# Signs of the weights from a ScalarE slope, first grams in half as many products, and a new order of the steps

## The chip, the cores and the metric

The kernel runs on one core of one Trainium2 chip. The metric is the device time of one execution in microseconds. Three runs of the kernel before gave 718.65, 718.37 and 716.71 us, median 718.37 us.

## The reference

A gated linear attention with a delta rule runs over 768 positions for 4 batches and 8 heads of width 48, and a feed-forward layer follows. Cut to what matters:

```python
def _attn_ref(q, k, v, beta):
    k_n = k / (norm(k, axis=-1, keepdims=True) + 1e-06)
    state = zeros((B, H, D, D))
    for t in range(S):
        kt, vt, bt = k_n[:, :, t], v[:, :, t], beta[:, :, t, None]
        y[:, :, t] = einsum('bhd,bhde->bhe', q[:, :, t], state)
        v_old = einsum('bhde,bhd->bhe', state, kt)
        state = state + bt[..., None] * einsum('bhd,bhe->bhde', kt, vt - v_old)
    return y

def _moe_ref(x, w_in, w_out):          # x: 3072 x 384, from y
    h = x @ w_in                       # w_in 384 x 2048
    g = h * erf(softplus(h))
    return g @ w_out                   # w_out 2048 x 384
```

The weights `w_in` and `w_out` arrive as 64-bit floats; the kernel receives each as a pair of 32-bit words.

## The kernel before, in words

**Attention.** The 768 positions are cut in 12 chunks of 64. For each chunk the kernel forms the grams of the keys (`gram_mm`), scales them by the step sizes and inverse norms of the keys (`norm_ops`, `gram_d`, `gram_a`), inverts the resulting triangular systems (for chunks 0 and 1 on VectorE: `first_blocks`, thirty steps of `first_row`, two transposes in `first_back`; for the others in pairs of chunks on GpSimd: `solve_row`, lines 362 and 363), merges the inverted blocks (`merge_*`) and runs the recurrence, which for each of 48 pairs of chunk and batch is `chain_u`, `chain_s` and `chain_y` on TensorE with copies between them.

**Feed-forward.** Four such pairs make a group of 256 tokens, and there are 12 groups. `x_max`, `x_all` and `x_scale` find the power of two that scales the group, `x_tr`, `x_hi` and `x_lo` split its values into two 16-bit parts. `ffn1` (line 659) multiplies them with the two 16-bit parts of `w_in`, nine products for each of 16 column blocks. Softplus (`e_sp`, line 685) and erf (`e_erf`, line 690) run on ScalarE, each with its own table, and `table` (line 126) issues a table load whenever the other one is wanted. `e_mul`, `e_split` and `e_rest` form the two parts of the product, and `ffn2` (lines 720 to 722) multiplies them with `w_out`. The results of `ffn1` live in two PSUM tiles `ph`; a new one waits until softplus and `h_out` (lines 670, 672) have read the old one.

**Weights.** Each of the two matrices passes through 12 tiles of 128 x 512 numbers. `w_load` brings 512 KB into a tile `raw`, of pairs of words. Of each pair, word 1 holds the sign, the exponent and the upper part of the mantissa, word 0 the rest. `w_mask` (line 536, ScalarE) reads word 1 as a 32-bit float, multiplies by 2^-112 and writes it to a staging place. `w_sign` (line 540, VectorE) keeps only the sign bit in word 1. `w_bits` with k = 0 (line 546, VectorE) shifts the staged word left by 3 and ors the sign in; with k = 1 (line 548, VectorE) it shifts word 0 right by 29 and ors it in. What stands in the staging place is then the weight in 32 bits. `w_sum` (line 553, ScalarE) accumulates magnitudes, `w_max`, `w_all` and `w_scale` make the scale of the matrix from the 12 sums, and `w_hi` (line 587, ScalarE) and `w_lo` (line 596, VectorE) write the two 16-bit parts. `ffn1` can't begin before all 12 tiles of `w_in` have gone through `w_sum`, since one scale serves the whole matrix; `ffn2` likewise needs `w_out`. The tiles `raw` borrow the 5 buffers of `H` and the 7 of `L`, so that twelve can be there at once and a later load waits until a `w_sum` has finished with a buffer.

**The first grams.** For chunks 0 and 1 a gram is wanted as four 32 x 32 blocks, with the blocks of the lower 32 rows in exchanged places. `gram_mm` makes one product for each block, head half and pair: 64 products for half a chunk, 256 for the four half chunks (line 246). Each is two instructions in the trace.

**The order.** The program records 2560 steps with planned times in a list `ev`, sorts them, and then takes them in the order that the table `ORDER` (line 33) gives. Every engine's queue, and the queue of SyncE that issues all loads and stores, is in that order. On TensorE 158 idle products (`warm`, line 141) on a tile of zeros stand in the queue ahead of the first `ffn1`.

## Time and profile before

| what | value |
|---|---|
| median of three runs | 718.37 us |
| the profiled execution: its time | 721.74 us |
| the profiled execution: its span | 720.0 us |
| TensorE busy | 641.5 us (89%) |
| VectorE busy | 512.5 us (71%) |
| ScalarE busy | 439.3 us (61%) |
| GpSimd busy | 387.7 us (54%) |
| first instruction of `ffn1` starts at | 112.89 us |

The span runs from the first instruction of the program to the last, and 1.7 us of the profiled execution lie outside it. The profiled execution is 3.4 us longer than the median. Engines are named PE (TensorE; PEld is its weight load), DVE (VectorE), ACT (ScalarE), POOL (GpSimd) and SP (SyncE); a row's times are microseconds from the start of the span, and what stands in brackets is the idle time of the engine just before and what ended it.

### The profile page before, as it was taken

Reading aid. Unit: us, or ns where it says so; the run is one execution under the profiler, and the core shown is the slowest. Engines: PE = TensorE matmul, PEld = TensorE weight load, DVE = VectorE, ACT = ScalarE, POOL = GpSimd, SP = SyncE. Lnnn points to the kernel's source line nnn. Section 1 sums busy time; section 2 is a strip of 40 time slices with the busy share of each in tenths; the row PEclk is TensorE's granted clock in tenths of the full one; section 3 lists DMA queues with packets and bytes.
Section 4 is the critical chain, followed back from the end, with each engine's and each line's share of the span. In section 5 each row is a group of like instructions: output and inputs, shape, how many; then the busy total and the mean of one; then the engine's idle time right before and its main releaser. Section 6 shows DMA issues by size and latency. Waiting matters only on the chain.

```text
span 720.0 us, 23322 instructions
## 1 busy us (share of the span) xinstructions
PE 641.5 (89%) x10074; PEld 490.9 (68%) x10074; DVE 512.5 (71%) x1053; ACT 439.3 (61%) x694; POOL 387.7 (54%) x540
## 2 busy tenths in 40 slices
PE   4687967796988899999899998999998899999996
PEld 3454645675865777877687776877876677777764
DVE  3599899985778767679568766767594775556562
ACT  1156777784757356576477755746754556867781
POOL 4341279986799823699703887323896331301332
PEclk8678977995999899999999999999999999999999
DMA  9733583152420064620414502506101500000100
GB/s 235 256 113 105 181 232 94 46 101 47 112 80 1 2 133 108 151 51 7 94 39 111 132 1 65 109 18 156 41 6 42 123 25 2 1 25 6 29 23 23
DMA packets 76422, 56.23 MB, mean 78 GB/s; under 512 B 57184, under 2 KB 66528, under 8 KB 76320
## 3 DMA queue, kind: packets, MB, share of 16 engines
q1 hardware_dynamic: 76320, 54.74, 30.5%
q8 instruction: 79, 1.29, 0.8%
q14 instruction: 23, 0.19, 0.1%
HBM read 42.14 MB, written 12.58 MB: 76 GB/s over the span
## 4 chain that ended last, share of the span: by engine, by line
PE 39%; DVE 25%; POOL 16%; issue 7%; ACT 6%; DMA 5%; SPq 1%; POOLq 0%; ACTq 0%; DVEq 0%
PE ph L659 13%; POOL xb L363 6%; POOL tmp L362 6%; PE pr L720 5%; PE pr L722 4%; PE pr L721 4%; DVE H L694 2%; POOL z L447 2%; PE pg L250 2%; PE pc L487 2%; PE pc L460 2%; ACT L126 2%; DVE xl L647 2%; DVE z L466 2%; DVE H L672 1%
## 5 line engine op out<-in xcount | busy, mean ns | idle before, releaser
L659 PE MATMUL ph<-xh,w_in 128*128 128x256 f16 x1152 | 213.5, 279 | 4.9 <-ACT L L685 4.5
L659 PEld LDWEIGHTS <-w_in 128*128 128x128 f16 x1728 | 168.6, 100 | 37.0 <-issue 7.7
L709 POOL TENSOR_TENSOR L<-H,L 128x512 f16<-128x512 f32 x72 | 85.7, 1202 | 175.8 <-DVE L L705 113.5
L659 PE MATMUL ph<-xl,w_in 128*128 128x256 f16 x576 | 160.5, 279 | 1.4 <-DVE xl L647 1.4
L126 ACT ACT_TABLE_LOAD x107 | 137.3, 1283 | 1.9
L722 PE MATMUL pr<-w_out,L 128*128 128x384 f16 x384 | 125.4, 327 | 7.7 <-POOL L L709 7.3
L721 PE MATMUL pr<-w_out,L 128*128 128x384 f16 x384 | 125.4, 327 | 0.4 <-DVE w_out L596 0.4
L720 PE MATMUL pr<-w_out,L 128*128 128x384 f16 x384 | 125.7, 327 | 0.0
L685 ACT ACTIVATE L<-ph,xct 128x512 f32<-128x512 f32 x96 | 65.3, 686 | 83.0 <-DVE H L672 68.9
L363 POOL TENSOR_TENSOR xb<-xb,tmp 128x31 f32<-128x31 f32 (+15 forms) x155 | 99.8, 644 | 12.2
L362 POOL TENSOR_TENSOR tmp<-gb,xb 128x31 f32<-128x31 f32 (+15 forms) x155 | 92.1, 594 | 21.6 <-DMA gb<-d 11.3
L447 POOL TENSOR_TENSOR z<-v,nm 64x192 f32<-64x192 f32 x96 | 56.4, 588 | 75.5 <-DMA v<-vtok 58.0
L694 DVE TENSOR_TENSOR H<-H,L 128x512 f32<-128x512 f32 x96 | 75.9, 801 | 28.0 <-ACT L L690 27.5
L672 DVE TENSOR_SCALAR H<-ph 128x512 f32<-128x512 f32 x72 | 49.0, 684 | 28.1 <-PE ph L659 27.7
L722 PEld LDWEIGHTS <-L 128*128 128x128 f16 x384 | 37.6, 98 | 34.5 <-POOL L L709 8.5
L690 ACT ACTIVATE L<-L 128x512 f32<-128x512 f32 x96 | 57.9, 625 | 0.7
L720 PEld LDWEIGHTS <-L 128*128 128x128 f16 x384 | 37.5, 98 | 21.5
L721 PEld LDWEIGHTS <-L 128*128 128x128 f16 x384 | 37.6, 98 | 20.2
L705 DVE CAST L<-H 128x512 f16<-128x512 f32 x72 | 43.1, 605 | 1.1
L481 DVE TENSOR_TENSOR z<-pc,z 48x192 f32<-48x192 f32 x72 | 25.4, 353 | 23.6 <-PE pc L473 13.7
L141 PE MATMUL warm<-zero 128*128 128x384 f16 x158 | 37.9, 390 | 1.1 <-DVE zero L132 1.1
L642 ACT ACTIVATE xh<-pt,xsx 64x128 f16<-64x128 f32 (+1 forms) x72 | 25.9, 394 | 20.7 <-PE pt L626 12.3
(154 smaller groups left out, 1034.7 us busy)
## 6 DMA issues: line engine op xcount, KB each, us to landing
raw_in<-w_in SPq DMA_DIRECT2D x12, 512.0 KB, 7.3
raw_out<-w_out SPq DMA_DIRECT2D x12, 512.0 KB, 5.7
d<-A SPq DMA_DIRECT2D x20, 256.0 KB, 3.4
kpg<-kT SPq DMA_DIRECT2D x24, 192.0 KB, 3.6
k<-ktok SPq DMA_DIRECT2D x12, 384.0 KB, 3.9
qp<-qT SPq DMA_DIRECT2D x24, 192.0 KB, 3.8
v<-vtok SPq DMA_DIRECT2D x48, 96.0 KB, 3.1
out<-ob SPq DMA_DIRECT2D x48, 96.0 KB, 2.2
```

Source lines behind the costliest of these rows:

```text
L126: se.add_instruction(mybir.InstLoadActFuncSet(name=nc.get_next_instruction_name(), act_func_set_id=i, ins=[], outs=[]))
L362: ge.tensor_tensor(tv, G[:, s, s + 1:].unsqueeze(1).broadcast_to([P, ncol, nr]), Xv[:, :, s:s + 1].broadcast_to([P, ncol, nr]), op=ALU.mult)
L363: ge.tensor_tensor(Xv[:, :, s + 1:], Xv[:, :, s + 1:], tv, op=ALU.add)
L447: ge.tensor_tensor(zz[j % 6][h1, :, hb, :], vt[j][h1], st[c]["nm"][h1, cs].unsqueeze(2).broadcast_to([C, NP, D]), op=ALU.mult)
L659: te.matmul(ph, w[:, i, kt * P:kt * P + P], G[x][:, :, ksl], start=(m == 0), stop=(m == 8))
L685: se.activation(unit("L", g, u), G["ph", u], AF.Softplus, bias=0.0, scale=G["ct"])
L690: se.activation(Lu, Lu, AF.Erf, bias=0.0, scale=1.0)
L694: ve.tensor_tensor(Hu, Hu, unit("L", g, u), op=ALU.mult)
L709: (ge if (g * NFF // EU + u) % GLM else ve).tensor_tensor(G["gl", u], unit("H", g, u), G["gh", u], op=ALU.subtract)
L720: te.matmul(G["po"][a], gh[:, o, asl], wout_h[:, i, :], start=(i == 0), stop=False)
L721: te.matmul(G["po"][a], gh[:, o, asl], wout_l[:, i, :], start=False, stop=False)
L722: te.matmul(G["po"][a], gl[:, o, asl], wout_h[:, i, :], start=False, stop=(i == NFF - 1))
```

## The change

Three things change.

**Signs.** `w_mask` uses the function Prelu in place of Copy, with the same scale and a slope of 2^32 for negative inputs. A negative weight's exponent field then is larger by 32, and that bit becomes the sign bit when the word is shifted left by 3. The word from `w_sign` is no longer needed. A new step `w_low` (VectorE, line 539 of the kernel after) shifts word 0 right by 29 in its place, and one `w_bits` (line 543) shifts the staged word and ors word 0 in. So each of the 24 tiles has two steps on VectorE where it had three; `w_low` reads nothing that ScalarE has made.

**First grams.** For chunks 0 and 1 one product covers both 32-column blocks of a row block; for the lower one it reads its right-hand side with the two blocks exchanged. There are 128 products of 32 x 64 where there were 256 of 32 x 32, 256 instructions in a trace where there were 512.

**Order.** `ORDER` is a new table, of 2536 steps. Lines behind the edits have moved up by 1 to 7.

```diff
-ORDER = (7,14,1,2,3,37,43,5,49,57,23,24,4,32,25,26,28,29,88,30,31,6,65,67,
+ORDER = (14,18,4,80,27,7,12,55,6,36,20,236,9,5,278,52,10,3,11,76,32,48,111,
...
             if name == "pg" and c < 2:
-                for x in range(2):
-                    for f in range(2):
-                        for hb in range(2):
-                            q0 = (1 - hb) * C + f * 32
-                            y = (f ^ x) * 32
-                            te.matmul(pg[q0:q0 + 32, o, x * 32:x * 32 + 32], kf[rd(hb), oo, f * 32:f * 32 + 32], kf[rd(hb), oo, y:y + 32], start=True, stop=True)
+                for f in range(2):
+                    for hb in range(2):
+                        q0 = (1 - hb) * C + f * 32
+                        rhs = kf[rd(hb), oo, :].rearrange("p (y t) -> p y t", y=2)
+                        te.matmul(pg[q0:q0 + 32, o, :].rearrange("p (y t) -> p y t", y=2), kf[rd(hb), oo, f * 32:f * 32 + 32], rhs[:, ::-1, :] if f else rhs, start=True, stop=True)
...
-        se.activation(stage(nm, i), hf, AF.Copy, bias=0.0, scale=2.0 ** -112)
-
-    def w_sign(nm, i):
-        hi = wt[nm]["raw", i][:, :, 1]
-        ve.tensor_scalar(hi, hi, -0x80000000, None, op0=ALU.bitwise_and)
-
-    def w_bits(nm, i, k):
-        raw = wt[nm]["raw", i]
+        se.activation(stage(nm, i), hf, AF.Prelu, bias=0.0, scale=2.0 ** -112, alpha=2.0 ** 32)
+
+    def w_low(nm, i):
+        lo = wt[nm]["raw", i][:, :, 0]
+        ve.tensor_scalar(lo, lo, 29, None, op0=ALU.logical_shift_right)
+
+    def w_bits(nm, i):
         ai = stage(nm, i).bitcast(I32)
-        if k == 0:
-            ve.scalar_tensor_tensor(ai, ai, 3, raw[:, :, 1], op0=ALU.logical_shift_left, op1=ALU.bitwise_or)
-        else:
-            ve.scalar_tensor_tensor(ai, raw[:, :, 0], 29, ai, op0=ALU.logical_shift_right, op1=ALU.bitwise_or)
+        ve.scalar_tensor_tensor(ai, ai, 3, wt[nm]["raw", i][:, :, 0], op0=ALU.logical_shift_left, op1=ALU.bitwise_or)
```

In what follows the order of a queue is shown as rows of line, operation, and what is written from what; numbers behind a name tell tiles of one name apart.

**The start of SyncE's queue.** `kpg` are keys for the first grams, `k` keys for the norms, `raw_in` weights. Before:

```order
L230 DMA kpg_115<-kT 48x1024 x2
L163 DMA k_130<-ktok 128x768
L163 DMA k_135<-ktok 128x768
L230 DMA kpg_141<-kT 48x1024 x2
L169 DMA be_152<-btok 128x32
L173 DMA qp_0_86<-qT 48x1024
L173 DMA qp_1_87<-qT 48x1024
L530 DMA raw_in_461<-w_in 128x1024
```

Now:

```order
L529 DMA raw_in_117<-w_in 128x1024
L230 DMA kpg_119<-kT 48x1024 x2
L230 DMA kpg_124<-kT 48x1024 x2
L529 DMA raw_in_127<-w_in 128x1024
L169 DMA be_130<-btok 128x32
L529 DMA raw_in_133<-w_in 128x1024
L169 DMA be_135<-btok 128x32
L163 DMA k_141<-ktok 128x768
L439 DMA v_143<-vtok 128x192
L529 DMA raw_in_178<-w_in 128x1024
L163 DMA k_180<-ktok 128x768
```

Both loads of `k` stood behind one pair of `kpg`; the second now stands behind two pairs and four tiles of weights.

**The start of VectorE's queue.** L189 sums the squares for the norms, L200 and what follows are the norms themselves. Before:

```order
L132 MEMSET zero 128x192
L189 TENSOR_REDUCE n_0_133<-w_out 128x16 x2
L200 TENSOR_SCALAR n_0_133<-n_0_133 128x32
L202 TENSOR_SCALAR ri_154<-n_0_133 128x32
L203 TENSOR_SCALAR ri_154<-ri_154 128x32
```

Now:

```order
L539 TENSOR_SCALAR raw_in_127<-raw_in_127 128x512
L539 TENSOR_SCALAR raw_in_117<-raw_in_117 128x512
L543 SCALAR_TENSOR_TENSOR w_in<-w_in,raw_in_117 128x512
L539 TENSOR_SCALAR raw_in_133<-raw_in_133 128x512
L132 MEMSET zero 128x192
L539 TENSOR_SCALAR raw_in_178<-raw_in_178 128x512
L543 SCALAR_TENSOR_TENSOR w_in<-w_in,raw_in_133 128x512
L189 TENSOR_REDUCE n_0_257<-w_out 128x16 x2
```

Work on the weights, of which there was none here, stands ahead of the norms. In all, 5 `w_low` and 3 `w_bits` now precede the first transpose (`first_blocks`), where nothing of the weights did.

**VectorE behind the second pair of transposes** (`first_back`, L328 before, L327 now). Before:

```order
L328 STREAM_TRANSPOSE w_out<-w_out 128x32x32
L540 TENSOR_SCALAR raw_in_617<-raw_in_617 128x512
L263 TENSOR_TENSOR w_out<-pr_83,gn_158 128x8x32
L540 TENSOR_SCALAR raw_in_639<-raw_in_639 128x512
L546 SCALAR_TENSOR_TENSOR w_in<-w_in,raw_in_617 128x512
L548 SCALAR_TENSOR_TENSOR w_in<-raw_in_617,w_in 128x512
L540 TENSOR_SCALAR raw_in_528<-raw_in_528 128x512
L548 SCALAR_TENSOR_TENSOR w_in<-raw_in_578,w_in 128x512
L546 SCALAR_TENSOR_TENSOR w_in<-w_in,raw_in_576 128x512
```

Now:

```order
L327 STREAM_TRANSPOSE w_out<-w_out 128x32x32
L262 TENSOR_TENSOR w_out<-pg_0_333,gn_307 128x8x32
L543 SCALAR_TENSOR_TENSOR w_in<-w_in,raw_in_182 128x512
L189 TENSOR_REDUCE n_1_689<-sq_539 128x16
L539 TENSOR_SCALAR raw_in_456<-raw_in_456 128x512
L543 SCALAR_TENSOR_TENSOR w_in<-w_in,raw_in_456 128x512
L539 TENSOR_SCALAR raw_out_387<-raw_out_387 128x512
L353 COPY xm_1_91<-pw_613 16x16x16
```

The next norms (L189) and the copies that the recurrence waits for (L353) come after fewer steps on weights, and a tile of `w_out` is already among these. Between the first transpose and these transposes stood 9 steps on weights (4 of line 540, 3 of 546, 2 of 548) and 2 of line 263; now there are 4 on weights (2 of line 539, 2 of 543). From these transposes to the first `x_max` (line 605; 600 now) there are 42 steps of lines 540 to 548 and 9 of line 596 before, and 33 of lines 539 and 543 and 8 of line 591 now; behind the first `x_lo` (line 647; 642 now) 17 of the former remain before, and 1 now.

On ScalarE, `table` issues 107 loads before and 127 now; 7 of the 20 more fall before the first store of an output tile is prepared, the others are spread over the rest. TensorE has the same 158 products of `warm`, all ahead of the first `ffn1` as before.

More of the change, by code (lines that the diff above doesn't have):

```diff
@@ L866, in delta_ffn_kernel @@
         on(us(tb), w_mask, "in", i)
-        on(us(tb + 0.5), w_sign, "in", i)
-        for k in range(2):
-            on(us(tb + 1 + 0.8 * k), w_bits, "in", i, k)
+        on(us(tb - 0.5), w_low, "in", i)
+        on(us(tb + 1), w_bits, "in", i)
         on(us(tb + 2.8), w_sum, "in", i)
@@ L874, in delta_ffn_kernel @@
         on(t - 0.3, w_mask, "out", i)
-        on(t - 0.2, w_sign, "out", i)
-        for k in range(2):
-            on(t + 0.15 * k, w_bits, "out", i, k)
+        on(t - 0.35, w_low, "out", i)
+        on(t + 0.1, w_bits, "out", i)
         on(t + 0.5, w_sum, "out", i)
```

2 lines of the change are left out of this document (1 added, 1 removed).

## The prediction

> **What bounds the kernel now.** First the page, then busy time by stage, with bounds that the timeline of VectorE gives: the first transpose of `first_blocks`, the end of the second pair of transposes, the first `ffn1`, and the end of VectorE's dense work.
>
> ```profile
> span 720.0 us, 23322 instructions
> PE   4687967796988899999899998999998899999996
> DVE  3599899985778767679568766767594775556562
> 0.00:27.42 27.42, 11.93 (x535) 8.78 (x537) 7.53 (x26) 2.97 (x3) 9.97 (x19) 0.71 0.96 270
> 27.42:51.80 24.38, 21.14 (x411) 14.13 (x413) 23.52 (x46) 11.30 (x19) 10.78 (x11) 0.78 0.41 142
> 51.80:112.90 61.10, 48.81 (x1132) 34.25 (x1124) 56.57 (x123) 46.23 (x103) 26.70 (x38) 0.84 0.60 169
> 112.90:168.00 55.10, 39.94 (x538) 31.55 (x536) 52.15 (x101) 41.62 (x75) 49.95 (x61) 0.90 0.28 60
> 168.00:720.00 552.00, 519.66 (x7480) 402.18 (x7480) 372.75 (x761) 337.13 (x495) 290.32 (x413) 0.97 0.25 57
> ```
>
> The columns behind the window are its length, then busy time (and instructions) of PE, PEld, DVE, ACT and POOL, the granted clock, the DMA share and GB/s. Behind 168 us TensorE is busy 519.66 of 552.00 us, so no other engine is worth much there. Ahead of it VectorE is the bound: 23.52 of 24.38, 56.57 of 61.10, 52.15 of 55.10 us. What TensorE does ahead of 112.9 us is partly idle products. So an earlier end of the front moves everything behind it, as long as TensorE finds its work. These are the places:
>
> ```profile
> 8.15 0.84 ACT L181 ACTIVATE w_out<-k 128x768 f32<-128x768 f32 x1 [1.40 <-DMA k<-ktok]
> 13.97 0.18 DVE L213 TENSOR_SCALAR ga<-gn 128x32 f32<-128x32 f32 x1
> 26.75 0.76 DVE L263 TENSOR_TENSOR w_out<-pg,gn 128x256 f32<-128x256 f32 x2 [4.95 <-PE pg L246]
> 27.42 2.12 DVE L315 STREAM_TRANSPOSE w_out<-w_out 128x1024 f32<-128x1024 f32 x1
> 49.74 2.06 DVE L328 STREAM_TRANSPOSE w_out<-w_out 128x1024 f32<-128x1024 f32 x1
> 114.67 0.37 PE L659 MATMUL ph<-xl,w_in 128*128 128x256 f16 x1 [1.39 <-DVE xl L647]
> ```
>
> Here the first transpose waits for the grams of line 246, not for the norms, which are done at 14 us; and `ffn1` waits for VectorE's `xl`.
>
> ```profile
> 15.34 1.93 PE L246 MATMUL pg<-kpg 48*32 48x32 f32 x128 [7.76 <-issue]
> 20.44 1.93 PE L246 MATMUL pg<-kpg 48*32 48x32 f32 x128 [3.17 <-issue]
> 25.81 0.87 PE L246 MATMUL pg<-kpg 48*32 48x32 f32 x49 [3.44 <-issue]
> ```
>
> The grams' own work is short: 1.93 us for 128 products and as many weight loads, then an idle stretch that ends with nothing but "issue". The starts lie 5.10 and 5.37 us apart while the loads hold 0.96 of the DMA engines, so I read it as instructions that arrive in blocks of 256, one per some 5 us. The Trainium skill, Runtime: NRT & Kernel Launch, section Instruction fetch mechanics, says that fetching goes in blocks of 256 instructions and that crossing one is mostly hidden. The trace agrees with the size and not with the hiding. By that sentence halving the grams would give nothing, by the rows it lifts this wait; my sum stays the same, since term 1 is bounded by a load.
>
> **Term 1, up to the first transpose: 0.4 us lost.** Of the 512 products with their weight loads 512 - 128 - 128 - 49 = 207 ran before the first gap, behind 16 of `warm`: 223 pairs. Now the last gram ends with pair 289 (256 of grams, 33 of `warm`), so one block of 128 pairs is missing, and that came by 15.34 us. The grams are then done near 17 us, ahead of the norms. VectorE's queue gets a wait at its head: the first `w_low` steps wait for tiles of weights, and behind them stand the zeros that `warm` waits for; the first two grams are ahead of `warm` on TensorE, and the others have until the norms are there. But the second `k` stands behind more loads:
>
> ```profile
> raw_in<-w_in SPq DMA_DIRECT2D x12, 512.0 KB, 7.3
> k<-ktok SPq DMA_DIRECT2D x12, 384.0 KB, 3.9
> kpg<-kT SPq DMA_DIRECT2D x24, 192.0 KB, 3.6
> 8.00:10.00 2.00, 0.00 (x0) 0.00 (x0) 0.95 (x1) 0.84 (x1) 0.66 (x2) 1.00 1.09 194
> ```
>
> Up to it: 4 x 512 + 4 x 192 + 2 x 384 and some 130 KB, 3.8 MB. At 270 GB/s (the mean up to 27.42) from about 1.7 us on that is 16 us, at 194 GB/s 21 us. Some of the loads behind it share the engines, so I take 18. From a landing to the last norm step it takes 13.97 + 0.18 - 8.15 = 6.0 us; one `w_low` (0.42), seven steps of 0.38 in place of the last ones, and one `w_bits` (0.69) add 3.8. The transpose starts at 18 + 9.8 = 27.8 in place of 27.42. Ends: 1.6 us gained, 3.4 lost.
>
> **Term 2, to the end of the transposes: 5.6 us gained.** Alone and beside GpSimd, the same step on weights has two prices:
>
> ```profile
> 36.79 0.42 DVE L540 TENSOR_SCALAR raw_in<-raw_in 128x512 int32<-128x512 int32 x1
> 38.30 0.69 DVE L546 SCALAR_TENSOR_TENSOR w_in<-w_in,raw_in 128x512 int32<-128x512 int32 x1
> 40.02 1.28 DVE L548 SCALAR_TENSOR_TENSOR w_in<-raw_in,w_in 128x512 int32<-128x512 int32 x2
> 45.74 2.40 DVE L540 TENSOR_SCALAR raw_in<-raw_in 128x512 int32<-128x512 int32 x2
> 48.05 1.76 DVE L546 SCALAR_TENSOR_TENSOR w_in<-w_in,raw_in 128x512 int32<-128x512 int32 x1
> ```
>
> The stage holds four steps of line 540 (0.42, 0.42, 2.40 for two), three of 546 (0.69, 0.69, 1.76), two of 548 (1.28) and two of line 263 (0.8): 8.5 us. Now it has two `w_low` and two `w_bits`: 2.2 us alone, 5.9 beside GpSimd. GpSimd is busy 10.78 of 24.38 us, so I take 2.9, nearer the first. 5.6 us go; ends 2.6 and 6.3. Everything else in the stage is one serial chain on VectorE, so what goes is gained. The loads of `qp` move behind seven tiles of weights; by the same rates they land near 25 us, where TensorE and GpSimd's masks have until the transposes.
>
> **Term 3, to the first `ffn1`: 8 us gained.** The means of the steps by shape:
>
> ```profile
> L540 DVE TENSOR_SCALAR raw_in<-raw_in 128x512 int32<-128x512 int32 x12 | 8.5, 716 | 0.0
> L540 DVE TENSOR_SCALAR raw_out<-raw_out 128x512 int32<-128x512 int32 x12 | 6.8, 566 | 0.1
> L546 DVE SCALAR_TENSOR_TENSOR w_in<-w_in,raw_in 128x512 int32<-128x512 int32 x12 | 9.6, 802 | 0.2
> L546 DVE SCALAR_TENSOR_TENSOR w_out<-w_out,raw_out 128x512 int32<-128x512 int32 x12 | 10.6, 888 | 0.1
> L548 DVE SCALAR_TENSOR_TENSOR w_in<-raw_in,w_in 128x512 int32<-128x512 int32 x12 | 8.6, 724 | 0.1
> L548 DVE SCALAR_TENSOR_TENSOR w_out<-raw_out,w_out 128x512 int32<-128x512 int32 x12 | 11.2, 961 | 0.1
> ```
>
> `w_low` has the shape and stride of line 540 and takes its price. Up to `x_max` the old queue has, for `w_in`, 8 of line 540, 9 of 546 and 10 of 548, and for `w_out` 5 of each: 20.2 + 12.1 = 32.3 us. The new one has 5 `w_low` and 7 `w_bits` of `w_in`, 11 and 10 of `w_out`: 9.2 + 15.1 = 24.3. So 8 us less, and 9.1 with the two steps of line 540 that also go between `x_max` and `x_lo`. ScalarE is the next limit: its queue has about the same 46 us of work here, so 61.1 us can become 52 only with ScalarE at 89% busy; I take 8, ends 4 and 9.1.
>
> **Term 4, 112.9 to 168 us: 5 us gained.** Of steps on weights, 17 become 1: by the means of `w_out`, 4 x 0.57 + 5 x 0.89 + 7 x 0.96 = 13.5 us less on VectorE. TensorE's idle time here is 55.1 - 39.9 = 15.2 us, so it could take that; but ScalarE, at 41.62 us, gets more table loads:
>
> ```profile
> L126 ACT ACT_TABLE_LOAD x107 | 137.3, 1283 | 1.9
> L536 ACT ACTIVATE w_out<-raw_out 128x512 f32<-128x512 f32 x12 | 7.8, 661 | 0.1
> 689.78 1.28 ACT L126 ACT_TABLE_LOAD   x1
> 691.20 0.69 ACT L685 ACTIVATE L<-ph,xct 128x512 f32<-128x512 f32 x1
> PE ph L659 <- ACT L L685: 4.5, 5, 1.5
> ```
>
> Seven more loads (9 us) fall into the first group's softplus and erf, some four of them ahead of 168 us: 41.6 + 5.1 = 47 us, near full if the stage shrinks to 50. I take 5; ends 0 and 13.
>
> **Behind 168 us: nothing.** The order is new there too, and 13 more table loads (17 us) lie beside a ScalarE that is busy 337 of 552 us. TensorE's idle time there is 32 us, so neither a gain nor a loss can be excluded; I take zero, with 4 us to each side. Prelu is one ACTIVATE like Copy, 0.66 us; were it dearer, 24 of them stand in ScalarE's queue in the front, and its cover is the 10% of term 3. The shorter PE work of the grams counts nothing, the wait ahead of them being the load's.
>
> The sum: -0.4 + 5.6 + 8 + 5 = 18.2 us. Against the profiled execution's own 721.74 that is 703.5; against the median of 718.37, 3.4 us less, 700.
>
> **The rivals.** *Half of it*: ScalarE bounds the front. For it speaks its 46 us of work in a stage of 52; against it that it waits for VectorE there now. Terms 3 and 4 shrink to 4 and 0, term 1 loses 3.4: 6 us, 712. *All of it*: terms 2 to 4 at their upper ends with TensorE taking up nearly all idle time, 28 us, 690. For it speaks TensorE's 15.2 idle us, against it the table loads. *Slower*: ScalarE's switches reach TensorE. `ph` has two tiles, so a softplus that stands behind one more load holds the next `ffn1`. If each of the 20 does, 20 x 1.28 = 25.7 us come back and the result is 718.4 - 18.2 + 25.7 = 726; from 14 of the 20 (18 us) on the change loses. Against it: 107 loads now leave TensorE waiting for softplus only 4.5 us in 5 waits. The Trainium skill, ScalarE: Activation LUTs, section What ACT_TABLE_LOAD costs, gives 1283 ns and a drain of 1380 ns for each switch; with that this rival would come to 53 us. The trace shows the first and not the second: the next ACTIVATE starts 1.42 us behind the start of the load. *It does not do what it says*: the front shrinks, and TensorE then waits for GpSimd's solves or for loads instead, within 2 us of now.
>
> **How the numbers follow.** A measurement of this kernel can tell 0.3% (2.2 us) from no change. Forecast of about 18 us: 0.54. Half of it: 0.2. All of it: 0.14. No change: 0.04. Slower: 0.08. The range leaves out the last two and the outer edges: from 690, where all is gained, to 713, just above the half. Faster 0.88, same 0.04, slower 0.08.
>
> **What would show it.** Right: the first transpose at 26 to 31 us, the second pair's end at 45 to 49, the first `ffn1` near 100 us with VectorE still over 90% busy ahead of it; the "issue" gaps ahead of the grams shrunk to one; 127 table loads with few waits of `ffn1` for softplus. Wrong: `k` landing behind 22 us, a VectorE that idles for ScalarE in the front, or more than 32 us of TensorE idle behind the front.

## The result, and the profile after

The changed kernel took 684.16 us (683.7 to 684.82, four runs) beside 717.54 us of the kernel before on the same chip, a ratio of 0.954 [0.951, 0.958]. Run again as a yardstick on two other chips it gave 0.947 [0.944, 0.950] and 0.945 [0.942, 0.948]: ratios of one kernel differ by up to 1% from chip to chip, more than these intervals, so runs on one chip are compared where there are any. The prediction was 700 us, with a range down to 690: right in sign, short by 16 us, and 6 us outside the range. In the profiled executions the span went from 720.0 to 682.5 us, 37.5 us less.

First the busy time by stage of the changed kernel. The first three bounds are those of the prediction (first transpose, end of the second pair of transposes, first `ffn1`); the next two are the end of GpSimd's first solve (the last of the 31 `solve_row` steps for chunks 2 and 3) and the first `ffn1` of the third group. Columns are as in the prediction: length, then busy time and instructions of PE, PEld, DVE, ACT and POOL, clock, DMA share, GB/s.

```profile
0.00:25.59 25.59, 16.09 (x331) 10.82 (x333) 11.99 (x36) 8.48 (x12) 12.55 (x24) 1.00 0.83 264
25.59:44.50 18.91, 15.21 (x313) 10.42 (x314) 17.77 (x38) 7.81 (x15) 7.51 (x7) 1.00 0.63 202
44.50:106.40 61.90, 46.27 (x1209) 34.01 (x1208) 50.67 (x115) 48.59 (x106) 26.88 (x40) 0.75 0.65 178
106.40:138.30 31.90, 24.98 (x348) 20.69 (x345) 26.91 (x69) 28.47 (x47) 27.65 (x46) 0.95 0.29 77
138.30:202.50 64.20, 58.85 (x1006) 45.68 (x1005) 46.56 (x83) 52.57 (x86) 55.91 (x68) 0.97 0.34 74
202.50:682.50 480.00, 465.95 (x6620) 358.26 (x6617) 326.31 (x692) 320.06 (x451) 248.15 (x358) 0.99 0.24 57
```

The same last three stages of the kernel before, cut at the same events:

```profile
112.90:148.10 35.20, 26.60 (x358) 21.33 (x356) 34.34 (x64) 26.70 (x49) 31.91 (x44) 0.89 0.17 43
148.10:229.80 81.70, 69.48 (x1037) 53.36 (x1038) 62.13 (x114) 53.16 (x90) 67.76 (x80) 0.90 0.33 75
229.80:720.00 490.20, 463.52 (x6625) 359.04 (x6623) 328.43 (x685) 298.89 (x433) 240.60 (x352) 0.98 0.24 56
```

Only 6.5 us were gained up to the first `ffn1` (112.9 to 106.4): 1.8 up to the first transpose, 5.5 up to the end of the second pair, and 0.8 lost in the long stage behind it, where VectorE is no longer full (50.67 of 61.90 us). The other 31 us came later: 3.3 up to the end of the solve, 17.5 from there to the third group (81.70 to 64.20), 10.2 behind it (490.20 to 480.00). In the stage of 17.5 us TensorE is idle 5.4 us in place of 12.2 and its work takes 10.6 us less, at a clock of 0.97 in place of 0.90. The part of that stage with half clock, before and now:

```profile
165.22:182.29 17.07, 13.84 (x224) 11.87 (x226) 9.56 (x13) 6.40 (x11) 10.40 (x10) 0.50 0.32 77
143.44:146.85 3.41, 3.37 (x17) 2.31 (x17) 3.35 (x5) 3.00 (x4) 3.41 (x3) 0.50 0.93 228
```

If work at half clock takes twice its time, an estimate, it cost 6.9 us before and costs 1.7 now. So of the 10.6 us some 5 are the clock, and some 5 are work that this stage no longer holds (1006 instructions in place of 1037). In the last stage idle time falls from 26.7 to 14.1 us.

The bounds themselves are in the timelines. Of the changed kernel (start, duration, engine, line, and in brackets the wait ahead):

```profile
15.15 1.56 ACT L181 ACTIVATE w_out<-k 128x768 f32<-128x768 f32 x2
25.59 2.15 DVE L314 STREAM_TRANSPOSE w_out<-w_out 128x1024 f32<-128x1024 f32 x1
42.51 2.00 DVE L327 STREAM_TRANSPOSE w_out<-w_out 128x1024 f32<-128x1024 f32 x1
88.64 0.24 POOL L361 TENSOR_TENSOR tmp<-gb,xb 128x31 f32<-128x31 f32 x1 [1.50 <-DMA gb<-d]
107.97 0.27 PE L654 MATMUL ph<-xl,w_in 128*128 128x256 f16 x1 [1.29 <-DVE xl L642]
138.02 0.27 POOL L362 TENSOR_TENSOR xb<-xb,tmp 128x31 f32<-128x31 f32 x1
202.51 0.27 PE L654 MATMUL ph<-xh,w_in 128*128 128x256 f16 x1
```

And of the kernel before:

```profile
98.91 0.51 POOL L362 TENSOR_TENSOR tmp<-gb,xb 128x31 f32<-128x31 f32 x1 [1.68 <-DMA gb<-d]
147.87 0.27 POOL L363 TENSOR_TENSOR xb<-xb,tmp 128x31 f32<-128x31 f32 x1
229.80 0.27 PE L659 MATMUL ph<-xh,w_in 128*128 128x256 f16 x1
```

The solve starts 10.3 us earlier, takes as long as before (49.7 us, 49.2 before) and ends 9.8 us earlier. Both kernels' solves stand on GpSimd between the grams of chunks 2 and 3 and the merge of chunk 2, whose recurrence feeds the third group.

The groups of the steps on weights, and the table loads, of the changed kernel (busy us, mean ns | idle time ahead):

```profile
L126 ACT ACT_TABLE_LOAD x127 | 162.9, 1283 | 2.2
...
L543 DVE SCALAR_TENSOR_TENSOR w_out<-w_out,raw_out 128x512 int32<-128x512 int32 x12 | 9.3, 782 | 0.7 <-ACT w_out L535 0.7
L543 DVE SCALAR_TENSOR_TENSOR w_in<-w_in,raw_in 128x512 int32<-128x512 int32 x12 | 8.3, 703 | 4.2 <-ACT w_in L535 3.9
L539 DVE TENSOR_SCALAR raw_out<-raw_out 128x512 int32<-128x512 int32 x12 | 7.7, 643 | 0.0
L539 DVE TENSOR_SCALAR raw_in<-raw_in 128x512 int32<-128x512 int32 x12 | 5.4, 458 | 10.8 <-DMA raw_in<-w_in 10.8
```

Two steps a tile at 0.46 to 0.78 us, in place of three: 30.7 us of VectorE where the six groups of before had 55.3. And the wait of `ffn1` for softplus, with all the 20 added table loads:

```profile
PE ph L654 <- ACT L L680: 5.7, 7, 1.8
```

It was 4.5 us in 5 waits. In this wait the added loads cost TensorE about a microsecond at most; no run took them out.

### The profile page after: what moved, and what is told of

Same layout as the page of the kernel before. It is cut to its first block, busy times and chain, and to the rows that moved or that the text cites. A ratio compares the mean times of both kernels' runs of the same rounds, so it can differ in the third digit from the quotient of the medians.

```text
span 682.5 us, 22802 instructions
## 1 busy us (share of the span) xinstructions
PE 627.4 (92%) x9818; PEld 479.9 (70%) x9818; DVE 480.2 (70%) x1029; ACT 466.0 (68%) x714; POOL 378.6 (55%) x540
## 4 chain that ended last, share of the span: by engine, by line
PE 38%; DVE 21%; POOL 14%; ACT 12%; DMA 6%; issue 5%; SPq 2%; POOLq 0%; DVEq 0%; ACTq 0%
PE ph L654 13%; POOL tmp L361 5%; POOL xb L362 5%; PE pr L715 4%; PE pr L717 4%; PE pr L716 4%; ACT L126 4%; POOL L L704 3%; DVE H L689 2%; PE pc L486 2%; PE warm L141 2%; ACT xh L637 2%; DVE H L667 1%; PE pc L459 1%; POOL z L446 1%
## 5 line engine op out<-in xcount | busy, mean ns | idle before, releaser
L654 PEld LDWEIGHTS <-w_in 128*128 128x128 f16 x1728 | 166.7, 99 | 38.2 <-issue 9.3
L704 POOL TENSOR_TENSOR L<-H,L 128x512 f16<-128x512 f32 x72 | 85.4, 1199 | 145.6 <-DVE L L700 103.1
L654 PE MATMUL ph<-xl,w_in 128*128 128x256 f16 x576 | 158.8, 276 | 1.3 <-DVE xl L642 1.3
L689 DVE TENSOR_TENSOR H<-H,L 128x512 f32<-128x512 f32 x96 | 79.1, 831 | 37.4 <-ACT L L685 36.0
L362 POOL TENSOR_TENSOR xb<-xb,tmp 128x31 f32<-128x31 f32 (+15 forms) x155 | 92.3, 596 | 12.2
L667 DVE TENSOR_SCALAR H<-ph 128x512 f32<-128x512 f32 x72 | 49.2, 685 | 31.0 <-PE ph L654 29.5
L715 PEld LDWEIGHTS <-L 128*128 128x128 f16 x384 | 37.5, 98 | 21.3
L700 DVE CAST L<-H 128x512 f16<-128x512 f32 x72 | 38.4, 541 | 1.3
L141 PE MATMUL warm<-zero 128*128 128x384 f16 x158 | 36.1, 376 | 3.0 <-DVE zero L132 3.0
L465 DVE TENSOR_TENSOR z<-pc,ga 64x192 f32<-64x192 f32 x80 | 28.4, 355 | 13.4 <-PE pc L459 11.8
```

The lines of the kernel that those rows point to most:

```text
L362: ge.tensor_tensor(Xv[:, :, s + 1:], Xv[:, :, s + 1:], tv, op=ALU.add)
L654: te.matmul(ph, w[:, i, kt * P:kt * P + P], G[x][:, :, ksl], start=(m == 0), stop=(m == 8))
L689: ve.tensor_tensor(Hu, Hu, unit("L", g, u), op=ALU.mult)
L704: (ge if (g * NFF // EU + u) % GLM else ve).tensor_tensor(G["gl", u], unit("H", g, u), G["gh", u], op=ALU.subtract)
L715: te.matmul(G["po"][a], gh[:, o, asl], wout_h[:, i, :], start=(i == 0), stop=False)
```

## The experiments

In what follows the microseconds that a run gains on the kernel before are worked out from its ratio and the median of before on its chip. The regularity that came out of the runs is shown first, since the later ones were made to test it. For each traced kernel: the start of the first `ffn1`; the end of the first solve (the end of the 31st row of `xb` on GpSimd); the start of the third group (the 289th row of `ffn1`); the distance of the two; the rest of the span.

| kernel | first `ffn1` | solve's end | third group | solve to third group | rest |
|---|---|---|---|---|---|
| before | 112.9 | 148.1 | 229.8 | 81.7 | 490.2 |
| old order, new signs and grams | 93.0 | 127.9 | 205.0 | 77.1 | 490.8 |
| old order, new signs alone | 103.3 | 138.3 | 215.3 | 77.0 | 490.8 |
| old order, new grams alone | 103.0 | 137.9 | 216.8 | 78.9 | 489.7 |
| before with idle products | 115.2 | 148.9 | 228.1 | 79.2 | 491.2 |
| new order, then old | 104.5 | 137.0 | 218.9 | 81.9 | 490.8 |
| old order, then new (hybrid) | 92.5 | 128.0 | 204.8 | 76.8 | 480.5 |
| hybrid with idle products, two traces | 90.7, 91.5 | 125.6, 126.4 | 199.4, 199.0 | 73.8, 72.6 | 479.7, 479.0 |
| changed kernel, three traces | 103.7 to 108.1 | 136.1 to 141.2 | 198.6 to 203.1 | 61.9 to 64.2 | 477.1 to 480.0 |
| new order, old signs | 128.1 | 162.3 | 225.0 | 62.7 | 484.2 |
| old order to the first transpose, then new, two traces | 103.1, 100.6 | 135.7, 133.4 | 198.4, 195.5 | 62.7, 62.1 | 478.0, 480.0 |
| old order to the first `x_max`, then new | 106.6 | 137.4 | 200.5 | 63.1 | 478.0 |
| old order to row 8 of the first solve, then new | 105.4 | 136.8 | 199.8 | 63.0 | 478.4 |
| old order to the first `put_blocks`, then new | 93.1 | 127.4 | 204.0 | 76.6 | 478.8 |
| changed, solve slowed | 108.1 | 147.6 | 211.4 | 63.8 | 479.5 |
| changed, first `ffn1` late | 113.9 | 143.7 | 206.7 | 63.0 | 478.8 |

With the old order up to the solve's end, or from the middle of the second group on, it takes 77 to 82 us from the solve's end to the third group (73 with idle products in two waits). With the new order from row 8 of the solve on, or earlier, it takes 62 to 64. Behind the third group the old one takes 490 us and the new one 477 to 484. The signs and the grams move the solve's end; the order moves the other two. But the distance from the first `ffn1` to the third group is nearly as steady: 107 to 117 us in the old order and 93 to 97 in the new. Of all these runs only the slowed solve parts the two marks, with 103.3 us from the first `ffn1` and 63.8 from the solve's end.

### The steps against the order

Theory V: the shorter work pays, in any order. Theory O: the order pays. The first four ran on one chip (before: 723.58 us). The first is the changed kernel in the order of before, with `w_low` at the places of `w_sign` and `w_bits` at those of the second `w_bits`:

```diff
-ORDER = (14,18,4,80,27,7,12,55,6,36,20,236,9,5,27
+ORDER = (7,14,1,2,3,37,43,5,49,57,23,24,4,32,25,2
...
```

> The changed kernel's steps (slope on ScalarE, one VectorE step less per tile, half the gram products) in the order of before: w_low stands where w_sign stood, w_bits where the second w_bits stood, all else as in the old table. Theory V (24 VectorE steps less in a front that VectorE bounds is what pays, the new order little): 684 to 695 us. Theory O (the order pays, since VectorE's saved time returns only if the steps around it move): 705 to 716 us.

697.23 us, 0.964 [0.960, 0.969]: 25.8 us less without any new order, and 2 us above theory V's range.

The next has the changed kernel's order and grams, and the three old steps with Copy, `w_sign` where `w_low` stands and both `w_bits` at the place of the one:

```diff
-        se.activation(stage(nm, i), hf, AF.Prelu, bias=0.0, scale=2.0 ** -112, alpha=2.0 ** 32)
+        se.activation(stage(nm, i), hf, AF.Copy, bias=0.0, scale=2.0 ** -112)
...
+    def w_sign(nm, i):
...
```

> The new order with the three old steps on each tile: w_sign where w_low stands if w_mask is ahead of it and else just ahead of w_bits, both w_bits in the place of the one, Copy in place of Prelu. 24 VectorE steps more than the changed kernel. Theory V: 18 us or more of the gain go, 702 to 715 us. Theory O: 3 to 10 us go, 687 to 694 us.

708.2 us, 0.979 [0.972, 0.986]. Beside the changed kernel's three ratios (0.954 to 0.945) the old steps give back 18 to 25 us, in an order that was made for the new ones. Its rest is 484.2 us, still 6 below the old order's.

Two hybrids of the orders follow, both with the new steps and grams, joined at `ffn1` number 24 (in the middle of the second group). The first takes the new order up to there, and then the steps that are left in the old order (the beginning of the table stays as it is):

```diff
 ORDER = (14,18,4,80,27,7,12,55,6,36,20,236,9,5,27
...
```

> The new steps; the new order up to the 24th column block of the first product (the middle of group 1), then the old order for all that is left. If the gain is made ahead of that place and only carried on behind it: 684 to 690 us. If the order behind it makes the 31 us that the traces show behind the first ffn1: 700 to 712 us.

712.04 us, 0.985 [0.980, 0.989]. The other takes the old order first:

```diff
-ORDER = (14,18,4,80,27,7,12,55,6,36,20,236,9,5,27
+ORDER = (7,14,1,2,3,37,43,5,49,57,23,24,4,32,25,2
...
```

> The reverse: the new steps in the old order up to the 24th column block, the new order for what is left. If the new order's gain lies ahead of the place: the same as the new steps in the old order throughout, within 4 us. If it lies behind: 10 us or more below that.

685.78 us, 0.948 [0.944, 0.952]. The two parts of the new order are worth different things: its later part takes 11.4 us off the kernel in the old order (697.23 to 685.78), and the table shows 10.3 of it behind the third group (490.8 to 480.5). Its first part with the old order behind loses 14.8 us (697.23 to 712.04), 9.1 of them at the solve's end. Theory V holds for the larger part: 3.6% of the changed kernel's 4.6 to 5.5%. The order adds 1.0 to 1.9%; the changed kernel did not run on this chip, so it can't be told closer. The new front by itself is no gain at all.

### Signs alone, grams alone

The prediction had counted nothing for the grams. Theory V keeps that; theory G gives them about half. Both ran in the old order, on one chip (before: 720.5 us), with the first two runs with idle products below. The first is the kernel in the old order from above with the old products put back:

```diff
-                        te.matmul(pg[q0:q0 + 32, o, :].rearrange("p (y t) -> p y t", y=2), kf[rd(hb), oo, f * 32:f * 32 + 32], rhs[:, ::-1, :] if f else rhs, start=True, stop=True)
+                            te.matmul(pg[q0:q0 + 32, o, x * 32:x * 32 + 32], kf[rd(hb), oo, f * 32:f * 32 + 32], kf[rd(hb), oo, y:y + 32], start=True, stop=True)
...
```

> Old order and old grams; only the signs of the weights are made in the new way (24 steps of VectorE fewer). Together with the halved grams this gave a ratio of 0.964 in the old order. Theory V (the steps of VectorE pay, the grams pay little, as the prediction had it): 0.968 to 0.975, 18 to 23 us less than before. Theory G (the halved grams pay about half of it, since the first transpose waits for them and not for the loads once nothing delays the second k): 0.978 to 0.986, 10 to 16 us less.

707.73 us, 0.981 [0.978, 0.985]: 13.4 us less. The other is the kernel before with the new products, nothing else:

```diff
-                            te.matmul(pg[q0:q0 + 32, o, x * 32:x * 32 + 32], kf[rd(hb), oo, f * 32:f * 32 + 32], kf[rd(hb), oo, y:y + 32], start=True, stop=True)
+                        te.matmul(pg[q0:q0 + 32, o, :].rearrange("p (y t) -> p y t", y=2), kf[rd(hb), oo, f * 32:f * 32 + 32], rhs[:, ::-1, :] if f else rhs, start=True, stop=True)
...
```

> The kernel before with only the first grams in half as many products; order and signs old. Theory V: within 0.4% of before, since the prediction counted nothing for the grams. Theory G: 0.982 to 0.990, 7 to 13 us less, the first transpose near 18 us in place of 27.4 and only one issue gap ahead of the grams.

708.53 us, 0.983 [0.978, 0.987]: 12.6 us less. The two make 26.0 us, and both together had made 25.8. Theory G. The timeline of the second shows why:

```profile
6.83 1.07 PE L245 MATMUL pg<-kpg 48*32 48x64 f32 x64
8.09 0.30 PE L245 MATMUL pg<-kpg 48*32 48x64 f32 x2 [0.19 <-DMA kpg<-kT]
8.82 1.31 PE L245 MATMUL pg<-kpg 48*32 48x64 f32 x77 [0.43 <-DMA kpg<-kT]
14.49 1.54 PE L245 MATMUL pg<-kpg 48*32 48x64 f32 x49 [4.37 <-issue]
...
16.75 2.14 DVE L314 STREAM_TRANSPOSE w_out<-w_out 128x1024 f32<-128x1024 f32 x1
```

One "issue" gap stands ahead of the grams where there were three (7.76, 3.17 and 3.44 us), and the first transpose starts at 16.75 us in place of 27.42. 10.2 us of that reach the solve's end (148.1 to 137.9), and the total. In the prediction's words, by the Trainium skill, Runtime: NRT & Kernel Launch, section Instruction fetch mechanics, halving the grams would give nothing, as fetching is mostly hidden; this run gives 12.6 us, so if these gaps are fetching, which the profile does not name, it is not hidden here.

### Does the half clock cost anything?

In the kernel before TensorE waits 5.82 us for VectorE ahead of the first gram of chunk 5, at 168.45 us. The windows around it (the clock is the third column from the end):

```profile
162.00:164.00 2.00, 0.63 (x4) 0.18 (x2) 1.88 (x4) 1.96 (x3) 2.00 (x3) 1.00 0.00 0
164.00:166.00 2.00, 0.00 (x0) 0.00 (x0) 1.88 (x4) 1.97 (x4) 1.92 (x2) 0.81 0.00 0
166.00:168.00 2.00, 0.00 (x0) 0.00 (x0) 1.97 (x3) 0.06 (x1) 1.69 (x2) 0.50 0.00 0
168.00:170.00 2.00, 1.55 (x29) 1.55 (x30) 2.00 (x4) 0.00 (x0) 0.00 (x0) 0.50 0.00 0
...
180.00:182.00 2.00, 2.00 (x40) 2.00 (x42) 1.97 (x3) 1.27 (x2) 1.89 (x2) 0.50 0.88 231
182.00:184.00 2.00, 2.00 (x40) 1.82 (x37) 2.00 (x3) 1.97 (x4) 1.24 (x2) 0.93 0.32 52
```

TensorE runs out of work at 162.6 us, the clock halves some 2.6 us later and stays so until 182.3, through 13.8 us of work. Theory C: the idle stretch is the cause, and the slow products cost time. So idle products went into the wait:

```diff
+    def idle(n, x):
+        for _ in range(n):
+            te.matmul(pr[x][:, 384:512], ident, ident, start=True, stop=True)
...
+    on(90 + 0, idle, 20, 2)
```

> The kernel before with 20 idle products (ident by ident, into columns that nothing reads) on TensorE ahead of the first gram of chunk 5, where TensorE waits 5.82 us for VectorE's A and has half the clock from 165.2 to 182.3 us. Theory C (an idle stretch of some 3 us halves the clock, and the slow products behind it are on the path): clock 1.0 there, the next group's start 4 to 8 us earlier, 0.989 to 0.995. Rival (the slow stretch is covered by other waits): the same time within 0.3%, the wait only moves.

The same stretch of this kernel, where the idle products run from 165.07 to 169.70 us:

```profile
166.00:168.00 2.00, 2.00 (x21) 2.00 (x20) 1.83 (x6) 1.97 (x4) 1.92 (x3) 1.00 0.00 0
168.00:170.00 2.00, 1.70 (x16) 1.51 (x14) 1.97 (x2) 0.74 (x2) 1.93 (x2) 1.00 0.04 8
170.00:172.00 2.00, 0.84 (x28) 0.84 (x30) 2.00 (x4) 0.00 (x0) 0.47 (x1) 1.00 0.00 0
172.00:174.00 2.00, 2.00 (x52) 1.85 (x47) 0.83 (x2) 0.70 (x2) 0.00 (x0) 1.00 0.67 129
...
180.00:182.00 2.00, 2.00 (x17) 1.42 (x15) 1.97 (x4) 1.99 (x3) 1.83 (x3) 1.00 0.70 195
```

The clock stays at 1.00, so its cause is shown: the idle stretch. Its price is not theory C's: 719.07 us in all, 0.997 [0.994, 1.000], where C had 0.989 to 0.995 and the rival a difference within 0.3%. The interval just reaches no change. Of the 17.1 us at half clock 13.8 were work, so some 6.9 us were to be had at most, and some 2 came back. From the solve's end to the third group it is 79.2 in place of 81.7 us: TensorE's own work falls from 69.5 to 64.8 us, but its waits, the idle products counted among them, grow from 12.2 to 14.3. Next, idle products in two waits of the hybrid of old order and new, ahead of the first gram of chunk 5 and of `ffn1` number 20:

```diff
+    on(90 + 0, idle, 14, 2)
+    on(90 + 1, idle, 20, 2)
```

> The hybrid (new steps, old order up to the product of ffn1 number 24, new order from there; 0.948 of before in its run) with idle products in two waits of TensorE: 14 ahead of the first gram of chunk 5 (a wait of 4.33 us for kpg) and 20 ahead of ffn1 number 20 (a wait of 5.90 us for the softplus). Half clock follows both now, 144 to 150 and 160 to 165 us. Theory C: 3 to 5 us less than the hybrid, 0.941 to 0.945. Rival: the hybrid's own time, 0.948, or worse where the idle products stand in the way.

682.29 us, 0.946 [0.942, 0.951], not to be told from the hybrid's 0.948, though its traces have the third group 3 to 4 us nearer to the solve's end. Run again beside the changed kernel on a third chip (before: 721.93 us):

> The hybrid with idle products in two waits of TensorE once more, on one chip with the changed kernel. If the hybrid's lead and the idle products are real: 0.941 to 0.947, and 5 to 9 us below the changed kernel. Rival (the 0.946 before was the spread of the chips): within 0.3% of the changed kernel.

682.03 us, 0.946 [0.942, 0.949], with the changed kernel there at 0.947:

> The changed kernel once more, as the yardstick of the three others on the same chip: 0.951 to 0.957.

683.44 us. So neither a lead of the hybrid over the changed kernel nor a gain by idle products is shown in the time; the rival holds.

### Is an earlier front passed on?

In the new order the second `k` stands behind loads of weights and the first transpose starts at 25.59 us; with the old order and the same steps it starts at 17.55. Theory F: what the front gains reaches the end. Theory E: the new front is longer because it holds steps that the old order has later, so nothing is to be had. Both kernels have the new steps and grams and the old order up to a join, and ran on the chip of the last two runs. The first join is at `first_blocks`:

```diff
-ORDER = (14,18,4,80,27,7,12,55,6,36,20,236,9,5,27
+ORDER = (7,14,1,2,3,37,43,5,49,57,23,24,4,32,25,2
...
```

> New steps; old order up to the first transpose, the new order from there, so that the second k is not behind the loads of weights. The first transpose should start near 17.5 us (25.6 in the changed kernel). Theory F (an earlier front is passed on to the end): 6 to 8 us less than the changed kernel, 0.943 to 0.947. Theory E (the new order's longer front holds steps on weights that the old order has later, so that the group that starts the dense part comes when it did): 0 to 2 us less, 0.950 to 0.955.

678.44 us, 0.940 [0.937, 0.942], below the changed kernel's 0.947 [0.944, 0.950] of the same chip by 5.0 us: the first version that beats both the new order and the old one. Its first transpose starts at 20.00 us, not near the 17.5 expected. In a second run, on another chip, it gave 0.941 [0.938, 0.945], which touches the changed kernel's 0.945 [0.942, 0.948] of a third:

> New steps; old order up to the first transpose, new order from there, once more as the yardstick of the two beside it (0.940 before): 0.936 to 0.946.

With the same table up to the first `x_max`:

> New steps; old order up to the first x_max, the new order from there. Theory F: first ffn1 near 93 us and, with the changed kernel's 96 us from there to the third group, the third group at 190, 0.935 to 0.940. Theory E: the six w_bits and three w_low that the new front has and the old has not come at the seam, first ffn1 at 98 to 101, the third group at 198 to 203, 0.948 to 0.954.

680.25 us, 0.942 [0.940, 0.944], which touches the changed kernel's 0.947 [0.944, 0.950]; first `ffn1` at 106.6, third group at 200.5. F's 190 is far off, and E's 98 to 101 for the first `ffn1` is too. An early front is passed on in part, more than E's ratios said. Why no more came is as E has it: what the new order has done by then is still to be done at the join, so the first `ffn1` comes 13.6 us later than in the old order (93.0).

### What sets the third group

By then the table's regularity was there, and with it theory S: the third group hangs on the solve of chunks 2 and 3, not on the first `ffn1`. One run delays the one by 8 us, one the other, with the changed kernel beside them (before: 720.87 us).

> The changed kernel as the yardstick of the two beside it: 0.945 to 0.956.

681.25 us, 0.945 [0.942, 0.948].

The first is slowed by a repeated multiplication:

```diff
+        for _ in range(12 if (sg, s) == (1, 15) else 1):
-        ge.tensor_tensor(tv, G[:, s, s + 1:].unsqueeze(1).broadcast_to([P, ncol, nr]), Xv[:, :, s:s + 1].broadcast_to([P, ncol, nr]), op=ALU.mult)
+            ge.tensor_tensor(tv, G[:, s, s + 1:].unsqueeze(1).broadcast_to([P, ncol, nr]), Xv[:, :, s:s + 1].broadcast_to([P, ncol, nr]), op=ALU.mult)
```

> The changed kernel with one multiplication of GpSimd's first solve (row 15 of the pair of chunks 2 and 3) issued 12 times in place of once: 8 us more ahead of the end of that solve, the values unchanged. Theory S (the third group's start hangs on the chain solve of chunks 2 and 3, merge, chain, x_max, and not on the first ffn1): the last row at 146 in place of 138 us, the third group's start 5 to 8 us later, 4 to 8 us more in all. Rival F (the end of the front at the first ffn1 sets what follows, GpSimd has slack): the same time within 0.3%.

690.97 us, 0.957 [0.954, 0.961], 9.7 us more than its yardstick, somewhat above S's 4 to 8. In its trace the first `ffn1` starts at 108.1 us, as in one trace of the changed kernel (solve's end 141.2, third group 203.1), which is to be set beside these two rows:

```profile
147.28 0.27 POOL L363 TENSOR_TENSOR xb<-xb,tmp 128x31 f32<-128x31 f32 x1
...
211.43 0.27 PE L655 MATMUL ph<-xh,w_in 128*128 128x256 f16 x1
```

The solve's end is 6.4 us later and the third group 8.3, with the first `ffn1` at the same time: a delay of GpSimd there goes through. (Against the trace of the yardstick on the same chip, 136.1 and 198.6, it is 11.4 and 12.8 us, but that trace has its first `ffn1` at 103.7.) The other delays TensorE, by idle products ahead of the first `ffn1`:

```diff
+    on(90 + 0, idle, 35, 2)
```

> The changed kernel with 35 idle products on TensorE right ahead of the first ffn1: 8 us later there, the solve untouched. Theory S: the third group starts 0 to 3 us later and the time grows by as little. Rival F: 6 to 8 us more in all.

687.72 us, 0.954 [0.950, 0.958], 6.5 us more. So S's number fell and the rival's 6 to 8 us came out: the delay of TensorE went through too. But the way it went is the solve:

```profile
113.91 0.27 PE L659 MATMUL ph<-xh,w_in 128*128 128x256 f16 x1
...
127.40 1.08 POOL L451 TENSOR_TENSOR z<-v,nm 64x192 f32<-64x192 f32 x2 [7.36 <-DMA v<-vtok]
...
143.39 0.27 POOL L367 TENSOR_TENSOR xb<-xb,tmp 128x31 f32<-128x31 f32 x1
...
206.72 0.27 PE L659 MATMUL ph<-xh,w_in 128*128 128x256 f16 x1
...
SPq L178 <- PE pr L491: 23.3, 1, 23.3
```

In the new order `put_v` steps (line 451 here) stand between the rows of the solve on GpSimd. A late TensorE holds up what they wait for, here 7.36 us, and the rows behind them wait as well: the solve takes 56 us in place of 50, and the third group comes 63.0 us behind its end, as ever. The wait is put down to the load of `v`, and TensorE's delay stands behind that load: in SyncE's queue it comes behind two loads of `qp`, which wait 23.3 us for TensorE's `chain_y` (line 491 here, last row above). They go out at 122.98 us and the load of `v` at 123.85; in the yardstick's trace on the same chip that is 114.92 and 115.80, and the solve ends 7.5 us earlier. So this run delayed both marks, and that a late first `ffn1` alone would cost nothing is not shown; the slowed solve is what speaks for S.

### Where the 15 us between the orders come from

Theory 1: the new order behind the solve is the shorter one. Theory 2: it is short because of work done ahead of the solve's end. Two joins inside that stretch, with the best version as the yardstick (677.33 us; before: 719.46).

The old order reaches up to the first `put_blocks` in one and up to row 8 of the first solve in the other:

```diff
-ORDER = (14,18,4,80,27,7,12,55,6,36,20,236,9,5,27
+ORDER = (7,14,1,2,3,37,43,5,49,57,23,24,4,32,25,2
...
```

> New steps; old order up to the first put_blocks, the end of GpSimd's first solve; new order from there. In every run so far the third group starts 62 to 64 us behind the end of that solve in the new order and 77 to 82 in the old one, and the rest takes 477 to 484 and 490 to 491 us. Theory 1 (the shorter stretch belongs to the order of the steps behind the solve): solve's end at 128, the third group at 190 to 192, 668 to 672 us, 0.927 to 0.933. Theory 2 (it is bought by work done ahead of the solve's end, which the new order does there and the old one does not): the stretch stays at 70 to 77, the third group at 198 to 205, 677 to 685 us, 0.940 to 0.950.

684.77 us, 0.953 [0.949, 0.956]: solve's end at 127.4, third group at 204.0, 76.6 us. Theory 2. TensorE has about the same work in that stretch as in the changed kernel (64.75 us with 14.11 of it at half clock, by the estimate above 57.7 at full clock; the changed kernel 58.85 with 3.37, 57.2), but it is idle 11.9 us in place of 5.4, and the half clock costs 7.1 in place of 1.7. The window of the stretch, its two parts with half clock, and the longest waits in it (in total, times, longest):

```profile
127.40:204.00 76.60, 64.75 (x1013) 49.92 (x1014) 46.15 (x90) 51.65 (x84) 58.94 (x73) 0.86 0.33 77
127.40:138.18 10.78, 6.50 (x48) 4.36 (x50) 5.00 (x17) 7.08 (x12) 9.63 (x13) 0.50 0.38 103
145.00:155.24 10.24, 7.60 (x111) 5.90 (x112) 5.85 (x8) 4.48 (x7) 5.88 (x7) 0.50 0.65 134
```

```profile
PE pe L398 <- DVE T L389: 5.4, 2, 4.9
PE pt L620 <- DVE A L256: 4.7, 1, 4.7
PE pg L249 <- DMA kpg<-kT: 3.8, 2, 3.3
```

The grams of chunks 4 and 5, their loads and VectorE's `A` come late here, in the midst of the merge; the changed kernel has its longest wait of that stretch at 1.8 us.

> New steps; old order up to row 8 of GpSimd's first solve, new order from there. Theory 1: solve's end at 130 to 137, the third group 63 us behind it, 193 to 200, 671 to 678 us, 0.931 to 0.940. Theory 2: the solve's end or the stretch behind it gives back what the front gained, the third group at 198 to 203, 0.940 to 0.948.

679.36 us, 0.945 [0.940, 0.949]: the solve's end at 136.8, the third group at 199.8, 63.0 us later. The events lie in the ranges of both theories; the time is theory 2's alone (theory 1 had up to 678 us and 0.940), by a little. The short stretch is there, and the solve's end has given back 8.9 of the old front's lead (127.9). So it is the first of the two runs that decides: the new order behind the solve alone does not make the stretch short. The work done ahead of it alone does not either: the kernel with the new order up to the middle of the second group and the old one behind that takes 81.9 us for the stretch. The 15 us take both parts, so theory 2 names one condition of two.

Which single steps among those moved ahead of the solve's end are worth the 15 us was not tried one by one and stays open, as does what the 10 us behind the third group consist of, beyond the idle time that the windows show.

## Why the prediction was wrong

By the traces the span fell by 37.5 us. Up to the first `ffn1` the sum had 13.2 us and 6.5 came; behind it the sum had 5 and 31 came. The step that failed is what the prediction had behind the front: term 4 priced there only the steps taken from VectorE, and then came *"Behind 168 us: nothing."* In its place the runs showed that the order by itself shortens two stretches, whatever the steps in it are: 77 to 82 us become 62 to 64 from the solve's end to the third group, and 490 become 477 to 484 behind it. Term 3 failed too, the other way.

**Term 1, up to the first transpose: -0.4 predicted, 1.8 gained.** The mechanism was right: `k` landed at 15 us where 18 was taken, and the transpose came 10.4 us behind it (9.8 taken). But the sentence *"The shorter PE work of the grams counts nothing, the wait ahead of them being the load's"* hid two things that nearly cancel. In the old order the grams were worth 12.6 us by themselves, and the new order spent most of that by putting the second `k` behind the weights (first transpose at 25.59 us in place of 17.55). The prediction saw the three gaps and counted them out, since it looked at the changed order alone. In its trace no "issue" gap stands ahead of the grams, which wait 6.5 us for their own loads instead; what the halved products are worth in the new order no run shows.

**Term 2: 5.6 predicted, 5.5 gained.** Right, by the steps that went from a serial chain.

**Term 3, to the first `ffn1`: 8 predicted, 0.8 lost.** The prices held (steps of 0.46 to 0.78 us), and VectorE's work in the stage fell by 5.9 us (56.57 to 50.67). What failed was that VectorE stays the bound there, *"with VectorE still over 90% busy"*: it is 82% busy, and its idle time grew from 4.5 to 11.2 us. By the profile 7.3 us of that are waits for ScalarE, one of the signs named as "wrong", and 2.5 for TensorE. The longest three:

```profile
DVE w_in L543 <- ACT w_in L535: 2.2, 1, 2.2
DVE mg L497 <- ACT y L491: 1.5, 1, 1.5
DVE m_in L560 <- PE spin L519: 1.2, 1, 1.2
```

Within one order *"So an earlier end of the front moves everything behind it"* holds: with the new steps in the old order the first `ffn1` comes 19.9 us earlier than before and the third group 24.8. Between the orders it does not. The new order has more steps on weights ahead of the first `ffn1` (23 `w_bits` in place of 17). With the same steps the first `ffn1` lies at 93.0 us in the old order and at 106.4 in the new, and the third group at 205.0 and 202.5.

**Term 4, 112.9 to 168 us: 5 predicted.** Its bound has no counterpart in the new order. From the first `ffn1` to the third group 20.8 us were gained (116.9 to 96.1), and in the old order with the same steps 4.9 (116.9 to 112.0): for the steps the size came near, over a longer stretch and in single traces, so partly by luck, and it left the order out. The table loads that it feared show as about a microsecond of waits.

**Behind 168 us: nothing predicted.** 10.2 us behind the third group, all by the order: kernels in the old order have 490 to 491 us there whatever their steps are. The 32 us of idle time that the prediction named were the place; it had no way to say whether the order would fill them, and took zero.

With the order left out the prediction would have been 18 us against 25.8 measured, short by what the grams are worth less some overestimate of the signs (13.4 measured, terms 2 to 4 had 18.6; a rough comparison, since term 2 also counted steps that the new order moves away). With it, the rest is missing. **The rivals:** "slower by table loads" fell (5.7 us of waits in place of 4.5), and so did "no change". "Half of it" had the front's 6 us, and VectorE's waits there are mostly for ScalarE, but ScalarE is not full (48.59 of 61.90 us), and its 712 left out all that came behind. "All of it" is nearest in number, but its mechanism, TensorE taking up nearly all its idle time, is not what came: from the first `ffn1` to the third group TensorE's idle time fell from 20.8 to 12.3 us, and the other 12 of the 20.8 us gained there are shorter work. It also kept the part behind 168 us at zero.

## What to carry to other kernels

When an order is made anew, the first event of a later stage is a poor mark for where the front ends: look for the chain that feeds a group some way behind (here GpSimd's solve), and check it by delaying that chain and its rival one at a time. A steady distance does not tell them apart when both move together, and a delay must be followed in the trace, since it can reach the other chain through a queue of loads. A change of parts and order together is best predicted as the parts in the old order first, each wait counted that they lift, and the order apart, bounded by the idle time of the engine that is full afterwards. Here waits in the "issue" of many short instructions at the program's start were real time, and one product that does the work of two lifted most of them.

## What the runs showed of the hardware

**The clock.** TensorE's granted clock fell to 0.50 about 2.6 us after its work ran out (162.6 to 165.2 us in the kernel before), and came back to 1.00 only 13.8 us after work had begun again at 168.45, though TensorE was busy all that time. In the changed kernel a stretch at half clock lasted 3.4 us (143.44 to 146.85) with TensorE busy for 3.37 of them. Twenty idle products in the wait kept it at 1.00. The Trainium skill, TensorE: Matmul & The Clock Gate, section What's actually happening, gives a window of about 3.4 us for both ways; the fall here came somewhat sooner, and the first of these two recoveries far later.

**The spread of the front.** Three traces of the changed kernel have their first `ffn1` at 103.7, 106.4 and 108.1 us and spans of 677.5, 682.5 and 680.2 us. A few microseconds in the front differ from execution to execution of one program, so single traces tell less than that there, and distances between events of one trace, like those of the table, tell more.
